# Expert weights prepared in single instructions, each behind the h of its group, and a third buffer for raw weights

## The chip, the cores and the metric

The program runs on one NeuronCore of a Trainium2 chip. The metric is the device time of one execution in microseconds (us). Three runs of the kernel before took 2126.69, 2133.93 and 2134.14 us (median 2133.93). The profile is that of one further execution, which took 2125.07 us.

Five engines work side by side, each through its own queue in order: PE (matrix multiply; PEld is its weight load), DVE (vector), ACT (activation), POOL (a second elementwise engine) and SP, which here only issues DMAs. An instruction that waits holds up all that stands behind it in its queue.

## The reference

Three layers follow one another on 2304 tokens of width 512: windowed attention, a feed-forward layer with a rational activation, and a mixture of eight experts in which every token goes through every expert:

```
P = exp(x @ w_gate - max);  8 times: P /= P.sum(1); P /= P.sum(0); P *= N / E
for e in range(8):
    h = maximum(x @ w1[e], 0)        # 512 -> 1024
    out += P[:, e:e+1] * (h @ w2[e]) # 1024 -> 512
```

The inputs and the output are float32, w1 and w2 have 2 MB each for an expert.

## The kernel before, in words

Only the expert stage, the last two thirds of the time, is touched by the change, with the end of the rational layer ahead of it.

**Groups.** The expert stage consists of 288 groups: eight experts, nine pairs of token tiles for each, four groups (i = 0 to 3) for each pair. In a group, `moe_l1` (L787) multiplies 256 tokens by two blocks of w1 in float16, each operand split into a high and a low half (24 matmuls of 256 columns, or 48 of 128 where the two tiles don't lie side by side: three pairs of the nine). `moe_a` then makes the group's h: ACT takes the relu (L804, four blocks of 128x128), POOL forms four sums and differences of the blocks (L806), ACT writes the high halves of the seven blocks that are used (L808) and DVE the low halves (L809, tile `hs`). `moe_l2` multiplies them by the prepared w2 of the group: seven block products instead of eight (`PRODS`), three matmuls each (L827 to L829), summed over i = 0 to 3 in four banks of PSUM. After the last group of a pair `y_evac` empties the four banks (ACT L860, DVE seven times L865) and adds the scaled result to the output tiles (DVE L873). All four banks are in use, so the next pair's first `moe_l2` waits for this evacuation bank by bank. In the code `moe_l2` runs two groups behind `moe_l1`.

**Preparation.** While one expert is computed, the next one's weights are made ready. Each of its eight raw tiles (128x1024 float32; k = 0 to 3 are w1, k = 4 to 7 are w2) is loaded twice. The first time DVE takes the largest absolute value (`raw_absmax`, L736). When all eight are done, `raw_scale` makes two powers of two from them. The second time the tile is split into float16 halves: for w1 one high half on ACT (L141) and one low half on DVE (L144); for w2 POOL first forms four differences of its quarters (L762, into the upper half of the tile `w4f`), then ACT and DVE split three raw quarters and the four differences apart. `raw_split` issues all of that for one tile in a row.

**Buffers.** The raw tiles share two buffers, tags `av0` and `av1`; a load is issued when the use two places ahead in the list `use` is issued. The prepared tiles rotate over six slots each for w1 and w2, four of which the running expert holds, so that i = 2 and 3 of the next expert can be written only after the running expert's last pair has used i = 0 and 1.

**Order.** The table `slots` (four slots to a group) sets the order in which the code issues the work, and `use` the groups at which the preparation is issued. The framework then schedules: it orders each engine's queue when the program is built, by a timeline of its own and by priorities, so an instruction that is issued late can be put earlier in its engine's queue where that timeline has a gap. Slots of the expert stage get a higher priority, those with `raw_absmax` and `raw_split` don't (`run_slot`, L997). Names that the prediction uses: "expert 0" to "expert 7" are the experts by number; the boundary between two experts is the first L827 of the later one.

Of the kernel before, what the change touches and what calls it, by code (L numbers as in the profile page):

```python
# [28 lines left out]
def kernel(  # L29
# [14 lines left out]
    nc = tc.nc  # L44
# [5 lines left out]
    P = 128  # L50
    KD = DM // P
# [15 lines left out]
    sb = ctx.enter_context(tc.tile_pool(name="sb", bufs=1))  # L67
# [551 lines left out]
    x2f, x2 = {}, {}  # L619
# [77 lines left out]
    NS1 = NB * NF1  # L697
# [16 lines left out]
    W1_AT = ("x1_1", "x1_2", "aqT", "aq", "ak", "x1_0")  # L714
    W2_AT = ("R0", "R1", "R2", "R3", "W5", "W6")
    ring = [0]

    def raw_load(e, k):
        t = sb.tile([P, 1024], F32, tag=f"av{ring[0] % 2}", name="wraw")
        ring[0] += 1  # L720
        w, i = divmod(k, NP)
        if w == 0:
            for h in range(2):
                nc.sync.dma_start(
                    out=t[:, h * DM:(h + 1) * DM].rearrange("p (k c) -> p k c", k=KD),
                    in_=bass.AP(w1.tensor, e * DM * FE + i * P + h * FH, [[FE, P], [P * FE, KD], [1, P]]),
                )
# [159 lines left out]
    LAG = 3  # L887
# [44 lines left out]
    after = []  # L932
# [24 lines left out]
    for n in range(NB):  # L957
        s = 4 * (SEQ.index((n, NF1 - 1, False, True)) + 1 + LAG)
# [11 lines left out]
    w4f = None  # L970
# [21 lines left out]
    for x, (s, fn, e, kx) in enumerate(use):
        at(s, fn, e, kx)
        if x + 2 < len(use):
            at(s, raw_load, *use[x + 2][2:])
# [129 lines left out]
```

## Time and profile before

| | |
|---|---|
| profiled execution | 2125.07 us, span 2123.2 us |
| PE busy | 2000.6 us (94% of the span) |
| DVE, ACT, POOL busy | 1343.0, 1022.7, 886.2 us (63%, 48%, 42%) |
| mean granted TensorE clock | 0.973 |
| DMA queue of the loads | 17.9% of the 16 engines' span |

PE's 94% is a mean over stages. The span in 40 slices (53 us each) shows PE at 6 to 8 tenths in the first five slices, where attention runs, and at 9 from there on; DVE at 8 or 9 in slices 4 to 12 and at 4 to 7 in the expert stage, which begins in slice 13. A matmul's row gives its start and a modelled end, and rows that follow each other overlap, so time that PE loses is read from the starts of rows, not from the busy share.

### The profile page before, as it was taken

How to read it: one execution, taken by the hardware profiler on the slowest of the kernel's cores; microseconds unless marked ns; L12 is line 12 of the kernel's file. 1: busy time of each engine (PE TensorE's matmuls, PEld its weight loads, DVE VectorE, ACT ScalarE, POOL GpSimd, SP SyncE). 2: the span in 40 equal slices, each digit the busy share in tenths (PEclk: the TensorE clock that was granted, in tenths of full speed). 3: DMA queues.
4: the chain of work that ended last, by engine and by line, in shares of the span. 5: the costliest groups of instructions: out<-in, count | busy, mean ns of one | idle time of the engine just before them, and what ended most of it. 6: DMA issues, size and time to landing. Idle time of an engine off the chain costs nothing.

```text
span 2123.2 us, 46647 instructions
## 1 busy us (share of the span) xinstructions
PE 2000.6 (94%) x19068; PEld 1744.0 (82%) x19068; DVE 1343.0 (63%) x2437; ACT 1022.7 (48%) x1981; POOL 886.2 (42%) x1471
## 2 busy tenths in 40 slices
PE   6688899999999999999999999999999999999998
PEld 5466678777778898989889888988988898899997
DVE  5799989989987635555554655455465555545444
ACT  5778777867863444334333333334333333334332
POOL 1222422212354534464453446455444645535333
PEclk7789999999999999999999999999999999999999
DMA  6642311131030104001210401121040112100000
GB/s 168 183 121 79 87 25 26 25 96 51 11 100 12 41 1 120 20 23 52 69 41 1 120 6 36 51 71 41 1 120 2 41 46 75 41 2 21 31 31 31
DMA packets 171654, 112.61 MB, mean 53 GB/s; under 512 B 74160, under 2 KB 156080, under 8 KB 171440
## 3 DMA queue, kind: packets, MB, share of 16 engines
q1 hardware_dynamic: 171440, 109.64, 17.9%
q8 instruction: 149, 2.44, 0.5%
q14 instruction: 65, 0.53, 0.1%
HBM read 104.88 MB, written 4.72 MB: 52 GB/s over the span
## 4 chain that ended last, share of the span: by engine, by line
PE 49%; DVE 10%; DMA 8%; POOL 5%; ACT 3%; issue 2%; SPq 1%; DVEq 0%; POOLq 0%; ACTq 0%
PE h2ps L787 25%; DMA wraw<-in_moe_w_dram 8%; PE yps L827 8%; PE yps L829 8%; PE yps L828 8%; POOL w L762 3%; DVE sm L736 2%; POOL ht L806 2%; DVE hs L809 1%; DVE ys L865 1%; ACT w1t L141 1%; DVE w1t L144 1%; DVE slab_q L576 1%; ACT hs L808 1%; DVE slab_t L588 1%
## 5 line engine op out<-in xcount | busy, mean ns | idle before, releaser
L806 POOL TENSOR_TENSOR ht<-ht 128x128 f32<-128x128 f32 x1152 | 590.6, 532 | 735.1 <-ACT ht L804 713.6
L787 PE MATMUL h2ps<-x,w1t 128*128 128x256 f16 (+1 forms) x9216 | 822.7, 247 | 0.0
L787 PEld LDWEIGHTS <-w1t 128*128 128x128 f16 x9216 | 721.0, 98 | 59.7 <-issue 0.8
L809 DVE TENSOR_TENSOR hs<-ht,hs 128x896 f16<-128x896 f32 x288 | 319.1, 1108 | 491.9 <-ACT hs L808 490.7
L827 PE MATMUL yps<-w2t,hs 128*128 128x256 f16 x2016 | 549.9, 274 | 43.5 <-DVE ys L865 39.9
L808 ACT ACTIVATE hs<-ht 128x896 f16<-128x896 f32 x288 | 273.2, 949 | 581.7 <-POOL ht L806 581.7
L828 PE MATMUL yps<-w2t,hs 128*128 128x256 f16 x2016 | 550.2, 274 | 0.0
L829 PE MATMUL yps<-w2t,hs 128*128 128x256 f16 x2016 | 547.4, 274 | 0.1
L804 ACT ACTIVATE ht<-h2ps 128x512 f32<-128x512 f32 x288 | 170.0, 590 | 237.1 <-PE h2ps L787 230.3
L828 PEld LDWEIGHTS <-hs 128*128 128x128 f16 x2016 | 197.8, 98 | 61.0 <-issue 38.2
L827 PEld LDWEIGHTS <-hs 128*128 128x128 f16 x2016 | 197.8, 98 | 33.0 <-ACT hs L808 10.6
L829 PEld LDWEIGHTS <-hs 128*128 128x128 f16 x2016 | 198.1, 98 | 24.4 <-DVE hs L809 0.6
L596 POOL TENSOR_TENSOR slab_g<-slab_t,slab_g 128x384 fp32r<-128x384 f32 x96 | 107.5, 1122 | 231.2 <-ACT slab_g L595 188.4
L865 DVE TENSOR_TENSOR ys<-yps,ys 128x256 f32<-128x256 f32 x468 | 167.2, 415 | 55.8 <-ACT ys L860 50.6
L611 PE MATMUL o1ps<-slab_g,wo_hi 128*128 128x384 f32 x384 | 139.3, 363 | 2.2 <-POOL slab_g L596 2.0
L558 PE MATMUL h1ps<-x,wi 128*128 128x384 f16 x384 | 129.4, 337 | 7.1 <-ACT p L316 4.9
L612 PE MATMUL o1ps<-slab_g,wo_lo 128*128 128x384 f32 x384 | 132.2, 344 | 0.0
L560 PE MATMUL h1ps<-x,wi 128*128 128x384 f16 x384 | 129.1, 336 | 1.0 <-DVE wi L144 0.8
L559 PE MATMUL h1ps<-x,wi 128*128 128x384 f16 x384 | 128.9, 336 | 0.0
L610 PE MATMUL o1ps<-slab_g,wo_hi 128*128 128x384 f32 x384 | 102.7, 368 | 13.7 <-ACT slab_g L595 13.2
L736 DVE TENSOR_REDUCE sm<-wraw 128x1 f32<-128x1024 f32 x64 | 77.9, 1216 | 51.1 <-DMA wraw<-in_moe_w_dram 51.0
L322 POOL TENSOR_TENSOR p<-p,sx 128x288 f32<-128x288 f32 x48 | 36.6, 762 | 128.2 <-DVE sx L321 95.7
(143 smaller groups left out, 2387.4 us busy)
## 6 DMA issues: line engine op xcount, KB each, us to landing
wraw<-in_moe_w_dram SPq DMA_DIRECT2D x192, 256.0 KB
wraw<-in_moe_w_dram SPq DMA_DIRECT2D x128, 128.0 KB
wst<-in_moe_w_in_dram SPq DMA_DIRECT2D x16, 512.0 KB
wost<-in_moe_w_out_dram SPq DMA_DIRECT2D x16, 512.0 KB
vst<-in_v_dram SPq DMA_DIRECT2D x6, 768.0 KB
out_dram<-acc SPq DMA_DIRECT2D x16, 256.0 KB
qks<-in_q_dram SPq DMA_DIRECT2D x16, 144.0 KB
qks<-in_k_dram SPq DMA_DIRECT2D x16, 144.0 KB
```

What stands on the lines that cost most here:

```text
L558: mm = nc.tensor.matmul(hp, whi, xb[:, 0, kk, :], start=kk == 0, stop=False)
L611: nc.tensor.matmul(ob[dd], hi, d["gl"], start=False, stop=False)
L612: nc.tensor.matmul(ob[dd], lo, d["gh"], start=False, stop=last)
L787: nc.tensor.matmul(hp[:, o:o + x.shape[-1]], w[:, wh, half, kk, :], x[:, xh, kk, :], start=half == 0 and kk == 0 and wh == 0 and xh == 0 a ...
L804: nc.scalar.activation(E[:, 0:4, :].rearrange("p n c -> p (n c)"), hp, AF.Relu)
L806: nc.gpsimd.tensor_tensor(out=E[:, o, :], in0=E[:, x, :], in1=E[:, y, :], op=op)
L808: nc.scalar.activation(hh, E[:, 1:8, :], AF.Copy)
L809: nc.vector.tensor_tensor(out=hl, in0=E[:, 1:8, :], in1=hh, op=ALU.subtract)
L827: nc.tensor.matmul(o, hh[:, a - 1, :], w[:, m, 0, :], start=i == 0 and half == 0, stop=False)
L828: nc.tensor.matmul(o, hh[:, a - 1, :], w[:, m, 1, :], start=False, stop=False)
L829: nc.tensor.matmul(o, hl[:, a - 1, :], w[:, m, 0, :], start=False, stop=i == NP - 1 and (half == 1 or b == 3))
L865: nc.vector.tensor_tensor(out=o, in0=s0, in1=s1, op=ALU.add)
```

## The change

`raw_split` no longer issues a tile's whole preparation. It returns a list of its single ACT and DVE instructions, which `raw_part` issues one at a time; POOL's differences are issued singly by `raw_diff`. Each of them, and each absolute maximum, gets a dependency (`pin`) on the latest instruction of the last `moe_a` on its own engine, so that the scheduler can't put it ahead of that group's h. The list of places is new: for the next expert the maxima are one to a group (before: one to a group and a half), the split starts two groups earlier and its parts are spread over several groups. From the raw tile number 20 on a third buffer, tag `x2f`, joins the two, and a load is issued at the use three places ahead. The arithmetic and the count of instructions on every engine are the same.

```diff
+    behind = {}
+    def pin(eng, i):
+        if eng in behind:
+            tc.add_manual_dep(i.ins, behind[eng], mybir.DependencyInfo(mybir.DependencyClass.Sync, mybir.DependencyReason.DATA), reason="after this group's h")
     def raw_load(e, k):
-        t = sb.tile([P, 1024], F32, tag=f"av{ring[0] % 2}", name="wraw")
+        n = ring[0]
         ring[0] += 1
+        tag = f"av{n % 2}" if n < 20 else ("av0", "av1", "x2f")[(n - 20) % 3]
+        t = sb.tile([P, 1024], F32, tag=tag, name="wraw")
...
     def raw_absmax(e, k):
-        nc.vector.tensor_reduce(out=rmx[:, k:k + 1], in_=raw.pop((e, k)), axis=AX, op=ALU.max, apply_absolute_value=True)
+        pin("v", nc.vector.tensor_reduce(out=rmx[:, k:k + 1], in_=raw.pop((e, k)), axis=AX, op=ALU.max, apply_absolute_value=True))
...
-            for o, x, y in ((d[:, 0], b[:, 0], b[:, 1]), (d[:, 1], b[:, 3], d[:, 0]), (d[:, 2], b[:, 3], b[:, 0]), (d[:, 3], b[:, 2], d[:, 1])):
-                nc.gpsimd.tensor_tensor(out=o, in0=x, in1=y, op=ALU.subtract)
-            split16(b[:, 1:4, :], t[:, 0:3, 0, :], t[:, 0:3, 1, :], e2[:, c:c + 1])()
-            split16(d, t[:, 3:7, 0, :], t[:, 3:7, 1, :], e2[:, c:c + 1])()
+            parts = [(b[:, 1:4, :], t[:, 0:3, 0, :], t[:, 0:3, 1, :], e2[:, c:c + 1]), (d, t[:, 3:7, 0, :], t[:, 3:7, 1, :], e2[:, c:c + 1])]
+        def hi(x, h, l, sc):
+            pin("a", nc.scalar.activation(h, x, AF.Copy, scale=sc))
+        def lo(x, h, l, sc):
+            pin("v", nc.vector.scalar_tensor_tensor(out=l, in0=x, scalar=sc, in1=h, op0=ALU.mult, op1=ALU.subtract))
+        return [lambda f=f, a=a: f(*a) for f in (hi, lo) for a in parts]
+    def raw_diff(e, i, o, x, y):
+        b = raw[e, NP + i].rearrange("p (n x) -> p n x", n=4)
+        d = w4f[:, 1024:2048].rearrange("p (n x) -> p n x", n=4)
+        pin("p", nc.gpsimd.tensor_tensor(out=d[:, o], in0=b[:, x], in1=d[:, y] if o % 2 else b[:, y], op=ALU.subtract))
...
-        nc.vector.tensor_tensor(out=hl, in0=E[:, 1:8, :], in1=hh, op=ALU.subtract)
+        behind["v"] = nc.vector.tensor_tensor(out=hl, in0=E[:, 1:8, :], in1=hh, op=ALU.subtract).ins.name
...
-        use += [(4 * (s0 + 3) + 6 * k + 1, raw_absmax, e, k) for k in range(8)]
-        use += [(4 * (s0 + s) + 1, raw_split, e, k) for s, k in ((18, 0), (20, 4), (22, 1), (24, 5), (33, 2), (35, 6), (36, 3), (37, 7))]
+        for i in range(8):
+            absmax_at(s0 + 4 * (4 + i) + 1, e, i)
...
+        split2_at(s0 + 4 * 36 + 3, e, 3, 1, s0 + 4 * 38 + 1, 1)
...
+    for x in range(2, len(use)):
+        s, e, kx, first = *use[x], begin[use[x]]
+        s = 4 * (NS1 + LAG + 3) if x == 22 else use[x - 2 if x < 22 else x - 3][0]
+        assert s < first
+        at(s, raw_load, e, kx)
```

What the scheduler makes of it is seen in the queues. First, DVE's queue at the boundary between experts 0 and 1, as it was: L809 is the low half of a group's h, L736 an absolute maximum for expert 2, L144 a low half of expert 1's last weights, L865 the evacuation of expert 0's last pair.

```order
L809 TENSOR_TENSOR hs<-ht,hs 128x896
L144 SCALAR_TENSOR_TENSOR w2t<-wraw,sm,w2t 128x3x256
L736 TENSOR_REDUCE sm<-wraw 128x1
L144 SCALAR_TENSOR_TENSOR w2t<-w_6335,sm,w2t 128x4x256
L736 TENSOR_REDUCE sm<-wraw 128x1
L809 TENSOR_TENSOR hs<-ht,hs 128x896
L736 TENSOR_REDUCE sm<-wraw 128x1
L865 TENSOR_TENSOR ys<-yps,ys 128x256
L865 TENSOR_TENSOR w_6335<-yps,ys 128x256
L865 TENSOR_TENSOR ys<-yps,ys 128x256 x2
L736 TENSOR_REDUCE sm<-wraw 128x1
L865 TENSOR_TENSOR acc_7138<-yps,ys 128x256
```

The same place in the changed kernel, where L835 is the h, L743 the maximum, L773 the low half of weights and L891 the evacuation:

```order
L773 SCALAR_TENSOR_TENSOR w2t<-w_6335,sm,w2t 128x4x256
L835 TENSOR_TENSOR hs<-ht,hs 128x896
L891 TENSOR_TENSOR ys<-yps,ys 128x256 x3
L891 TENSOR_TENSOR w_6335<-yps,ys 128x256
L891 TENSOR_TENSOR acc_7138<-yps,ys 128x256
L891 TENSOR_TENSOR w_6335<-yps,ys 128x256
L891 TENSOR_TENSOR acc_7138<-yps,ys 128x256
L835 TENSOR_TENSOR hs<-ht,hs 128x896 x2
L773 SCALAR_TENSOR_TENSOR w2t<-wraw,sm,w2t 128x3x256
L773 SCALAR_TENSOR_TENSOR w2t<-w_6335,sm,w2t 128x4x256
L835 TENSOR_TENSOR hs<-ht,hs 128x896 x2
L743 TENSOR_REDUCE sm<-wraw 128x1
```

The maxima have left the boundary: the first one stands behind the h of the new expert's fifth group, and nothing stands between the h and the evacuation of the old expert's last pair.

Second, POOL's queue where the first two w2 tiles of expert 1 are prepared during expert 0, as it was (L806 are the sums of h, four to a group; L762 the differences of raw weights):

```order
L806 TENSOR_TENSOR ht<-ht 128x128 x45
L762 TENSOR_TENSOR w_6335<-wraw 128x256 x2
L762 TENSOR_TENSOR w_6335<-wraw,w_6335 128x256
L806 TENSOR_TENSOR ht<-ht 128x128 x2
L762 TENSOR_TENSOR w_6335<-wraw,w_6335 128x256
L806 TENSOR_TENSOR ht<-ht 128x128 x5
L762 TENSOR_TENSOR w_6335<-wraw 128x256 x2
L806 TENSOR_TENSOR ht<-ht 128x128
L762 TENSOR_TENSOR w_6335<-wraw,w_6335 128x256 x2
```

And as it is in the changed kernel (L831 for h, L780 for the differences):

```order
L831 TENSOR_TENSOR ht<-ht 128x128 x64
L780 TENSOR_TENSOR w_6335<-wraw 128x256
L780 TENSOR_TENSOR w_6335<-wraw,w_6335 128x256
L831 TENSOR_TENSOR ht<-ht 128x128 x4
L780 TENSOR_TENSOR w_6335<-wraw 128x256
L780 TENSOR_TENSOR w_6335<-wraw,w_6335 128x256
L831 TENSOR_TENSOR ht<-ht 128x128 x20
L780 TENSOR_TENSOR w_6335<-wraw 128x256
L780 TENSOR_TENSOR w_6335<-wraw,w_6335 128x256
```

Differences now come two at a time behind a whole h and no longer split one; before, three came in a row and three more stood inside the four sums of two groups.

Third, DVE's queue at the end of the rational layer (L578 to L588 are its elementwise steps), as it was:

```order
L586 SCALAR_TENSOR_TENSOR slab_q<-slab_q,slab_a 128x384
L587 SCALAR_TENSOR_TENSOR slab_a<-slab_q,slab_a 128x384
L736 TENSOR_REDUCE sm<-wraw 128x1
L587 SCALAR_TENSOR_TENSOR slab_a<-slab_q,slab_a 128x384
L588 SCALAR_TENSOR_TENSOR slab_t<-slab_t,sm,slab_a 128x384
L119 TENSOR_REDUCE sm<-sm 128x1
L588 SCALAR_TENSOR_TENSOR slab_t<-slab_t,sm,slab_a 128x384
L736 TENSOR_REDUCE sm<-wraw 128x1 x2
L809 TENSOR_TENSOR hs<-ht,hs 128x896
```

And in the changed kernel:

```order
L586 SCALAR_TENSOR_TENSOR slab_q<-slab_q,slab_a 128x384
L587 SCALAR_TENSOR_TENSOR slab_a<-slab_q,slab_a 128x384
L588 SCALAR_TENSOR_TENSOR slab_t<-slab_t,sm,slab_a 128x384
L835 TENSOR_TENSOR hs<-ht,hs 128x896 x2
L639 TENSOR_REDUCE sm<-x2f 128x1
L773 SCALAR_TENSOR_TENSOR w2t<-wraw,sm,w2t 128x3x256
L773 SCALAR_TENSOR_TENSOR w2t<-w_6335,sm,w2t 128x4x256
L105 TENSOR_REDUCE sm<-mxps 128x1
```

All eight maxima for expert 1, and the last w2 tile of expert 0, stood in the rational layer; the maxima now stand in expert 0, one behind each h from its fifth group on, and the w2 tile behind the first two h. Ahead of the first of these maxima the queues are the same.

## Rows read from the trace of the kernel before

**Rows 1.** Waits of PE, 620 us to the end: us in total, times, longest
```profile
PE yps L827 <- DVE ys L865: 39.9, 21, 4.2
```

**Rows 2.** Busy time by stretch, experts 0, 1, 6, 7: start:end, length, PE, PEld, DVE, ACT, POOL, clock
```profile
637.16:827.48 190.32, 181.19 (x1933) 164.18 (x1934) 110.39 (x219) 81.01 (x114) 89.45 (x160) 0.98 0.12 36
827.48:1014.61 187.13, 180.15 (x1912) 163.54 (x1912) 98.17 (x152) 70.04 (x96) 91.83 (x160) 0.99 0.16 47
...
1762.59:1946.51 183.92, 181.48 (x1912) 164.34 (x1911) 94.93 (x151) 68.54 (x93) 90.17 (x160) 0.98 0.10 31
1946.51:2123.20 176.69, 169.87 (x1838) 155.28 (x1835) 74.69 (x122) 56.79 (x78) 63.06 (x137) 0.99 0.08 28
```

**Rows 3.** Timeline, undisturbed groups of expert 1: start, us, engine, line, tiles, idle before
```profile
872.41 2.84 PE L787 MATMUL h2ps<-x,w1t 128*128 128x128 f16 x48
877.38 2.78 PE L787 MATMUL h2ps<-x,w1t 128*128 128x256 f16 x24
880.87 1.81 POOL L806 TENSOR_TENSOR ht<-ht 128x128 f32<-128x128 f32 x4 [3.10 <-ACT ht L804]
882.29 2.78 PE L787 MATMUL h2ps<-x,w1t 128*128 128x256 f16 x24
882.72 0.95 ACT L808 ACTIVATE hs<-ht 128x896 f16<-128x896 f32 x1 [1.92 <-POOL ht L806]
883.70 1.09 DVE L809 TENSOR_TENSOR hs<-ht,hs 128x896 f16<-128x896 f32 x1 [3.82 <-ACT hs L808]
...
885.11 0.60 ACT L804 ACTIVATE ht<-h2ps 128x512 f32<-128x512 f32 x1 [1.45 <-PE h2ps L787]
...
886.18 2.61 DVE L865 TENSOR_TENSOR ys<-yps,ys 128x256 f32<-128x256 f32 x7 [1.39 <-ACT ys L860]
```

**Rows 4.** Timeline, DVE and PE at the boundary of experts 0 and 1
```profile
823.75 1.22 DVE L736 TENSOR_REDUCE sm<-wraw 128x1 f32<-128x1024 f32 x1 [1.48 <-DMA wraw<-in_moe_w_dram]
...
827.01 0.42 DVE L865 TENSOR_TENSOR ys<-yps,ys 128x256 f32<-128x256 f32 x1
827.48 0.37 PE L827 MATMUL yps<-w2t,hs 128*128 128x256 f16 x1 [4.22 <-DVE ys L865]
```

**Rows 5.** Busy time by stretch, the same boundary
```profile
820.00:830.00 10.00, 5.78 (x43) 4.53 (x42) 7.23 (x10) 4.10 (x6) 6.68 (x12) 0.84 0.70 206
```

**Rows 6.** Timeline, POOL, ACT and PE where expert 2's weights are split
```profile
902.73 3.19 POOL L762 TENSOR_TENSOR w<-wraw 128x256 f32<-128x256 f32 x2 [1.42 <-DMA wraw<-in_moe_w_dram]
...
908.86 1.15 ACT L141 ACTIVATE w2t<-w,sm 128x1024 f16<-128x1024 f32 x1 [4.22 <-POOL w L762]
...
912.98 0.27 PE L827 MATMUL yps<-w2t,hs 128*128 128x256 f16 x1 [2.24 <-DVE ys L865]
```

**Rows 7.** Timeline, DVE and PE at the start of the expert stage
```profile
637.21 1.22 DVE L736 TENSOR_REDUCE sm<-wraw 128x1 f32<-128x1024 f32 x1 [3.84 <-DMA wraw<-in_moe_w_dram]
...
637.16 0.28 PE L827 MATMUL yps<-w2t,hs 128*128 128x256 f16 x1 [2.34 <-ACT hs L808]
```

**Rows 8.** Busy time by stretch: five gate groups of expert 0; two stretches of the rational end
```profile
664.68:690.24 25.56, 25.56 (x332) 24.12 (x331) 19.92 (x58) 8.12 (x11) 8.87 (x20) 1.00 0.01 2
588.00:629.80 41.80, 39.90 (x257) 30.69 (x254) 41.44 (x58) 25.49 (x48) 18.35 (x17) 1.00 0.35 104
609.59:634.70 25.11, 23.08 (x158) 19.02 (x155) 21.14 (x31) 12.72 (x26) 8.29 (x12) 1.00 0.43 128
```

**Rows 9.** Groups by line, all absolute maxima of raw weights: count, busy us, mean ns
```profile
L736 DVE TENSOR_REDUCE sm<-wraw 128x1 f32<-128x1024 f32 x64 | 77.9, 1216 | 51.1 <-DMA wraw<-in_moe_w_dram 51.0
```

**Rows 10.** Timeline, first issue of a raw w2 tile on SP, and the maximum that reads it
```profile
829.97 0.34 SPq L730 DMA_DIRECT2D wraw<-in_moe_w_dram  x1
...
834.24 1.22 DVE L736 TENSOR_REDUCE sm<-wraw 128x1 f32<-128x1024 f32 x1 [2.23 <-DMA wraw<-in_moe_w_dram]
```

**Rows 11.** Timeline, a difference on POOL alone; an h on DVE beside one
```profile
908.11 0.72 POOL L762 TENSOR_TENSOR w<-wraw,w 128x256 f32<-128x256 f32 x1
...
903.84 1.50 DVE L809 TENSOR_TENSOR hs<-ht,hs 128x896 f16<-128x896 f32 x1
```

More of the change, by code (lines that the diff above doesn't have):

```diff
@@ L749, in raw_split @@
         w, i = divmod(k, NP)
-        slot = (e * NP + i) % 6
         c = e % 2
@@ L753, in raw_split, with raw_part @@
         if w == 0:
-            t = w1s[e, i] = sb.tile([P, 2, 2, KD, P], F16, tag=W1_AT[slot], name="w1t")
+            t = w1s[e, i] = sb.tile([P, 2, 2, KD, P], F16, tag=W1_AT[(e * NP + i) % 6], name="w1t")
             v = t.rearrange("p s h k c -> p s (h k c)")
-            split16(src, v[:, 0, :], v[:, 1, :], e1[:, c:c + 1])()
+            parts = [(src, v[:, 0, :], v[:, 1, :], e1[:, c:c + 1])]
         else:
-            t = w2s[e, i] = sb.tile([P, 7, 2, EH], F16, tag=W2_AT[slot], name="w2t")
+            t = w2s[e, i] = sb.tile([P, 7, 2, EH], F16, tag=W2_AT[(e * NP + i) % 6], name="w2t")
             b = src.rearrange("p (n x) -> p n x", n=4)
             d = w4f[:, 1024:2048].rearrange("p (n x) -> p n x", n=4)
-            for o, x, y in ((d[:, 0], b[:, 0], b[:, 1]), (d[:, 1], b[:, 3], d[:, 0]), (d[:, 2], b[:, 3], b[:, 0]), (d[:, 3], b[:, 2], d[:, 1])):
-                nc.gpsimd.tensor_tensor(out=o, in0=x, in1=y, op=ALU.subtract)
-            split16(b[:, 1:4, :], t[:, 0:3, 0, :], t[:, 0:3, 1, :], e2[:, c:c + 1])()
-            split16(d, t[:, 3:7, 0, :], t[:, 3:7, 1, :], e2[:, c:c + 1])()
+            parts = [(b[:, 1:4, :], t[:, 0:3, 0, :], t[:, 0:3, 1, :], e2[:, c:c + 1]), (d, t[:, 3:7, 0, :], t[:, 3:7, 1, :], e2[:, c:c + 1])]
[8 more added lines that the diff above has]
+        pin("p", nc.gpsimd.tensor_tensor(out=d[:, o], in0=b[:, x], in1=d[:, y] if o % 2 else b[:, y], op=ALU.subtract))
+    DIFFS = ((0, 0, 1), (1, 3, 0), (2, 3, 0), (3, 2, 1))
+    todo_w = {}
+    def raw_part(e, k, n):
+        if (e, k) not in todo_w:
+            todo_w[e, k] = raw_split(e, k)
+        for _ in range(n):
+            todo_w[e, k].pop(0)()
     def x2_tile(tt):
@@ L805, in moe_a @@
         for o, x, y, op in ((4, 0, 2, ALU.add), (5, 4, 1, ALU.subtract), (6, 1, 0, ALU.subtract), (7, 3, 5, ALU.subtract)):
-            nc.gpsimd.tensor_tensor(out=E[:, o, :], in0=E[:, x, :], in1=E[:, y, :], op=op)
+            i = nc.gpsimd.tensor_tensor(out=E[:, o, :], in0=E[:, x, :], in1=E[:, y, :], op=op)
+        behind["p"] = i.ins.name
         hh, hl = hs[st % 3]
-        nc.scalar.activation(hh, E[:, 1:8, :], AF.Copy)
-        nc.vector.tensor_tensor(out=hl, in0=E[:, 1:8, :], in1=hh, op=ALU.subtract)
+        behind["a"] = nc.scalar.activation(hh, E[:, 1:8, :], AF.Copy).ins.name
+        behind["v"] = nc.vector.tensor_tensor(out=hl, in0=E[:, 1:8, :], in1=hh, op=ALU.subtract).ins.name
         cur[NS1 + st] = hh, hl
@@ L976, with used, absmax_at, split1_at @@
     at(4 * 87, w4_alloc)
-    use = [(4 * (65 + k) + 1, raw_absmax, 0, k) for k in range(8)]
-    use += [(4 * (74 + i) + 1, raw_split, 0, i) for i in range(4)]
-    use += [(4 * s + 1, raw_split, 0, 4 + i) for i, s in enumerate((88, 90, 93, 96))]
+    use, begin = [], {}
+    def used(s0, s, e, kx):
+        use.append((s, e, kx))
+        begin[s, e, kx] = s0
+    def absmax_at(s, e, k):
+        at(s, raw_absmax, e, k)
+        used(s, s, e, k)
+    def split1_at(s, e, i, gap):
+        at(s, raw_part, e, i, 1)
+        at(s + gap, raw_part, e, i, 1)
+        used(s, s + gap, e, i)
+    def split2_at(s, e, i, step, t, gap):
+        for n, d in enumerate(DIFFS):
+            at(s + n * step, raw_diff, e, i, *d)
+        at(t, raw_part, e, NP + i, 1)
+        at(t + gap, raw_part, e, NP + i, 1)
+        at(t + 2 * gap, raw_part, e, NP + i, 1)
+        at(t + 3 * gap, raw_part, e, NP + i, 1)
+        used(s, t + 3 * gap, e, NP + i)
+    for i in range(8):
+        absmax_at(4 * (65 + i) + 1, 0, i)
+    for i in range(4):
+        split1_at(4 * (74 + i) + 1, 0, i, 1)
+    for i, x in enumerate((88, 90, 93, 96)):
+        split2_at(4 * x + 1, 0, i, 0, 4 * x + 1, 1)
     at(4 * 69, raw_scale, 0, 0)
@@ L984 @@
     for e in range(1, NE):
-        s0 = NS1 + (e - 1) * EB
-        use += [(4 * (s0 + 3) + 6 * k + 1, raw_absmax, e, k) for k in range(8)]
-        use += [(4 * (s0 + s) + 1, raw_split, e, k) for s, k in ((18, 0), (20, 4), (22, 1), (24, 5), (33, 2), (35, 6), (36, 3), (37, 7))]
-        at(4 * (s0 + 15), raw_scale, e, 0)
-        at(4 * (s0 + 15) + 1, raw_scale, e, 1)
-    for _, _, e, kx in use[:2]:
-        at(4 * 62, raw_load, e, kx)
[L992 to L995, printed above, removed]
+        s0 = 4 * (NS1 + (e - 1) * EB)
+        for i in range(8):
+            absmax_at(s0 + 4 * (4 + i) + 1, e, i)
+        at(s0 + 4 * 14, raw_scale, e, 0)
+        at(s0 + 4 * 14 + 1, raw_scale, e, 1)
+        split1_at(s0 + 4 * 16 + 1, e, 0, 4)
+        split2_at(s0 + 4 * 17 + 1, e, 0, 2, s0 + 4 * 19 + 3, 2)
+        split1_at(s0 + 4 * 22 + 1, e, 1, 4)
+        split2_at(s0 + 4 * 23 + 1, e, 1, 2, s0 + 4 * 25 + 3, 2)
+        split1_at(s0 + 4 * 33 + 1, e, 2, 3)
+        split2_at(s0 + 4 * 32 + 1, e, 2, 2, s0 + 4 * 35 + 1, 1)
+        split1_at(s0 + 4 * 34 + 3, e, 3, 3)
+        split2_at(s0 + 4 * 36 + 3, e, 3, 1, s0 + 4 * 38 + 1, 1)
+    for _, e, kx in use[:2]:
+        at(4 * 62, raw_load, e, kx)
+    use.sort(key=lambda u: u[0])
+    for x in range(2, len(use)):
[3 more added lines that the diff above has]
+        at(s, raw_load, e, kx)
     def run_slot(s):
         for fn, a in slots.pop(s, ()):
-            early = fn is run_piece or fn is flush or (s >= 4 * NS1 and fn not in (raw_absmax, raw_split))
+            early = fn is run_piece or fn is flush or (s >= 4 * NS1 and fn not in (raw_absmax, raw_part, raw_diff))
             with tc.high_priority(offset=400) if early else ExitStack():
```

## The prediction

> **What bounds the kernel now.** I read the waits of PE first. In the expert stage almost all of them are one kind: the first L827 of a pair waits for DVE to empty the PSUM banks, 21 times, 39.9 us [rows 1]. Then I cut the stage at each expert's first L827 [rows 2]. Expert 7, during which nothing is prepared, takes 176.69 us with the end of the program in it; experts 1 to 6 (six of one pattern, the first and last are shown) take 183.92 to 187.63, together 1946.51 - 827.48 = 1119.03 us.
>
> The timeline gives what an undisturbed expert costs. Group starts lie 877.38 - 872.41 = 4.97 us apart with 128-column matmuls and 882.29 - 877.38 = 4.91 with 256 columns, and PE shows no wait there [rows 3]. An expert has 12 of the one and 24 of the other: 59.64 + 117.84 = 177.5 us. So experts 1 to 6 lose 1119.03 - 6 x 177.5 = 54.0 us, 9.0 each. Expert 0 takes 190.32; when it starts, four h2 blocks are already multiplied instead of the usual three, so its clean time is 177.5 - 2.7 = 174.8 and it loses 15.5. Only part of this is idle time: in the 10 us around the boundary PE is busy for 5.78 and the granted clock has a mean of 0.84, so after the wait PE runs a while at the lower of its two levels, 1.2 GHz [rows 5].
>
> Two places in an expert make the loss. At the boundary DVE stands at an absolute maximum whose tile hasn't landed (1.48 us at 823.75); the h and the evacuation are queued behind it, the evacuation starts at 827.01, and PE has waited 4.22 us by 827.48 [rows 4]. About 85 us later POOL waits 1.42 us for a raw tile and takes the first two differences in 3.19 us, ACT waits 4.22 us for the last, with the next relu behind it in its queue, and PE loses 2.24 us [rows 6].
>
> **The room in an undisturbed group** [rows 3], on which the rest hangs. The h that starts at 877.38 is finished by DVE at 883.70 + 1.09 = 884.79; PE uses it after the h2 blocks of the next two groups, at about 882.29 + 4.91 + 2.6 = 889.8. That is 5.0 us of room. The evacuation starts at 886.18 and frees the first bank after one of its seven instructions (2.61 / 7 = 0.37), needed at the same 889.8: room about 3.2 us. DVE is free from 884.79 to 886.18, ACT from 883.67 to 885.11, and POOL idles 3.10 us before each h.
>
> **The change part by part.** It adds and removes no instruction, so each edit is a shift.
>
> *Maxima behind h, one to a group.* One takes 1.22 us [rows 9] and fits into DVE's 1.39 us ahead of the evacuation; in the three groups of four without evacuation there is more. What is late next if its tile isn't there: the evacuation, from 1.39 + 3.2 - 1.22, about 3.4 us on. The tile is loaded three uses ahead: 3 x 4.91 - 1.22 = 13.5 us between the release of its buffer and its use. In the trace SP's first issue and the use are 834.24 - 829.97 = 4.3 us apart, with DVE waiting at the end of them [rows 10]. So 9 us are to spare, and the boundary's wait should go. SP's own queue holds only these loads, in the order of use, so a late release delays the later ones too; each has the same spare time.
>
> *Splits as single instructions.* DVE's part (up to 1.5 us) fits like a maximum. A high half on ACT takes 1.15 us [rows 6] against 1.44 free. In two groups of an expert two come in a row, so the next relu is some 0.7 us late, of 5.0. The worst group on DVE, the one ahead of the boundary, has three low halves behind one h, about 3.8 us; they end about where the next h is ready. Two differences on POOL take 1.44 us at their shortest [rows 11] and 3.19 at their longest [rows 6], against 3.10 idle.
>
> *The end of the preparation.* The last w2 tile is now ready behind the h of group 38 of an expert's count, about three groups later than before; PE uses it at group 41. By the times above DVE is through some 10 us after group 38 starts and PE comes 17 us after it: 7 us to spare.
>
> *Bound of these.* Nothing in the trace shows a prepared expert without a loss, so I bound what stays in experts 1 to 6: nothing at one end, 4 us each (one wait of the size at 827.48) at the other. I take 1 us each, near the clean row, since every piece is smaller than its gap; two small matmuls for the scales are in it. Gain 54.0 - 6 = 48.0 us.
>
> *Expert 0.* The maxima for expert 1 now share DVE with the gate iterations. Five such groups keep DVE busy for 19.92 of 25.56 us without them [rows 8]; five maxima add 6.1, 26.0 in all, so DVE is full there and PE must wait a little. Bounds: 0 and the 6 us of the maxima; I take 3, and 2 more for matmuls of gate and logits that are real work (an estimate from that window: 25.56 against 5 x 4.93 = 24.7, so 0.9 in five groups). The start of the stage loses its bubble, its scale and its boundary waits. Gain 15.5 - 5 = 10.5, between 6 and 14.
>
> *End of the rational layer.* DVE is busy 41.44 of 41.80 us there [rows 8]. Six maxima (7.3 us) and a w2 tile leave this stretch, and two more that held the first h back, one for 3.84 us [rows 7]. PE can win its 25.11 - 23.08 = 2.0 us of idle time [rows 8] and the 2.34 us ahead of 637.16 [rows 7]: at most 4.4. It could also be nothing, if ACT's and POOL's steps are as late as DVE's. I take 3.
>
> Sum: 48.0 + 10.5 + 3 = 61.5 us off 2125.07, so 2063.5. The three runs shown lie 1.6 to 9.1 us above the profiled execution; with waits for DMA gone I expect less scatter, and forecast **2066 us** as a median.
>
> **The lock of a port.** A difference alone takes 0.72 us; beside it an h on DVE takes 1.50 instead of 1.09 [rows 3, 11]. So POOL and DVE hold each other up, and the pins put the differences just where DVE runs its h. This is rival C. The Trainium skill ("SBUF — State Buffer", SBUF: two separate sides) says that GpSimd and a VectorE instruction with two SBUF inputs take a shared pair of ports as an exclusive lock for a whole instruction and the loser blocks; these rows agree as far as they go.
>
> **The rivals.**
> A, the forecast: the waits go, 2050 to 2080. Chance 0.76.
> B, a wait in place of the one removed: DVE or a late tile still holds up one evacuation per expert, 3 to 5 us each instead of 9. For it: DVE's queue is still in order and every part still waits for others. Against: 9 us of spare time for the tile. 2066 + 6 x 3 + 4 = 2088, between 2080 and 2105. Chance 0.13.
> C, the lock: per expert 16 differences lose up to 0.7 us and 12 low halves up to 0.4, some 16 us; if three fifths of it reached PE the gain would be gone: 7 x 9.6 = 67, so 2066 + 67 = 2133. It decides only from 3.2 us of delay in one group; two differences and one low half give at most 1.8. Chance 0.03.
> D, the preparation does not do what it says, since the scheduler's order meets late tiles elsewhere: about 2125 to 2140. The queues speak against it. Chance 0.03.
> E, slower: the last w2 tile comes after its use. It has 7 us to spare; each us beyond costs PE 7 us in all, so it eats the gain from 7 + 61.5 / 7 = 16 us of delay and at 20 us gives 2066 + 7 x 13 = 2157. For it: this tile is now prepared three groups later. Against: nothing in rows 3 or 10 is late by a third of that. Chance 0.05.
>
> **How the numbers follow.** Within 0.5% (10.7 us, about what a measurement here can tell from no change) lie C and D: same 0.05, a little of D on the slower side; E and that: slower 0.05; A and B: faster 0.90. The range: below, no waits at all and the full start, 2125.07 - 54 - 13.5 - 4.4 + 2 = 2055, and some runs under it: 2049. Above, it takes in the middle of B: 2094. A and the lower part of B hold about 0.82.
>
> **What would show it.** Right: experts 1 to 6 at 178 to 179 us each, the waits of L827 for L865 under 8 us in all, the maxima of L743 without waits for DMA, clock 1.00 at the boundaries, first L853 some 3 us earlier. Wrong: an evacuation still late at an expert's start (B), differences of 1.4 us and more in every pair (C), L853 waiting for `w2t` near group 41 (E). An expert 0 above 185 us would show the gate iterations' crowding as the next bound.

## The result and the profile after

Four runs of the changed kernel took 2059.31, 2061.48, 2061.65 and 2063.64 us, median **2061.57**; the kernel before took 2130.36 in the median of its four. The ratio is 0.967 (95% interval 0.966 to 0.969). The forecast was 2066. The profiled execution took 2059.31 us (span 2057.4), 65.8 less than that of before.

The waits of PE from 620 us to the end, in the changed kernel (us in total, times, longest):

```profile
PE smps L109 <- DVE gs L681: 1.5, 3, 0.7
PE yps L853 <- DVE ys L891: 0.2, 1, 0.2
```

The second row answers to [rows 1]: 39.9 us have become 0.2. The first is new, the small matmuls of the gate in expert 0 that wait for DVE. The stage cut at the experts' first L853, for experts 0, 1 and 6 (columns as in [rows 2]; expert 7, to the end, takes 176.64 us), with the 10 us around the boundary in front:

```profile
805.00:815.00 10.00, 10.00 (x94) 8.96 (x93) 6.48 (x10) 4.37 (x7) 8.34 (x14) 1.00 0.38 106
631.86:812.13 180.27, 178.73 (x1934) 162.59 (x1932) 111.74 (x226) 80.27 (x114) 84.92 (x159) 1.00 0.18 51
812.13:990.15 178.02, 178.02 (x1915) 162.95 (x1912) 100.28 (x150) 71.61 (x95) 86.26 (x160) 1.00 0.17 49
1702.35:1880.76 178.41, 178.18 (x1915) 162.89 (x1913) 103.09 (x155) 70.66 (x93) 88.88 (x161) 1.00 0.15 43
```

PE has no gap across the boundary and its granted clock is 1.00, where [rows 5] had 5.78 us of 10 and 0.84. Experts 1 to 6 take 178.02 to 178.41 us. The timeline around the boundary, DVE, POOL, ACT and PE of the changed kernel:

```profile
802.47 1.28 DVE L773 SCALAR_TENSOR_TENSOR w1t<-wraw,sm,w1t 128x1024 f16<-128x1024 f32 x1
803.68 1.01 DVE L773 SCALAR_TENSOR_TENSOR w2t<-wraw,sm,w2t 128x768 f16<-128x768 f32 x1
803.88 3.47 POOL L831 TENSOR_TENSOR ht<-ht 128x128 f32<-128x128 f32 x4 [3.55 <-ACT ht L829]
804.61 1.48 DVE L773 SCALAR_TENSOR_TENSOR w2t<-w,sm,w2t 128x1024 f16<-128x1024 f32 x1
807.38 0.95 ACT L834 ACTIVATE hs<-ht 128x896 f16<-128x896 f32 x1 [3.58 <-POOL ht L831]
...
808.36 1.55 DVE L835 TENSOR_TENSOR hs<-ht,hs 128x896 f16<-128x896 f32 x1 [2.28 <-ACT hs L834]
...
809.84 1.27 DVE L891 TENSOR_TENSOR ys<-yps,ys 128x256 f32<-128x256 f32 x3
...
812.13 0.27 PE L853 MATMUL yps<-w2t,hs 128*128 128x256 f16 x1
...
819.30 1.28 DVE L773 SCALAR_TENSOR_TENSOR w2t<-w,sm,w2t 128x1024 f16<-128x1024 f32 x1
...
826.87 0.27 PE L853 MATMUL yps<-w2t,hs 128*128 128x256 f16 x1
```

Here the three low halves stand behind one h, the crowded group of the prediction. Beside them POOL's four sums take 3.47 us instead of 1.81 [rows 3], and still the evacuation starts 2.3 us ahead of PE's use at 812.13: the matmul's row has no wait. Where [rows 4] had a maximum and its missing tile, nothing stands between the h and the evacuation. The last two rows give the spare time of the last w2 tile: ready at 819.30 + 1.28 = 820.58, used at 826.87, so 6.3 us.

### The profile page after: what moved, and what is told of

It reads as the page before. It is cut to its first block, busy times and chain, and to the rows that moved or that the text cites. A ratio compares the mean times of both kernels' runs of the same rounds, so it can differ in the third digit from the quotient of the medians.

```text
span 2057.4 us, 46783 instructions
## 1 busy us (share of the span) xinstructions
PE 1982.5 (96%) x19068; PEld 1738.1 (84%) x19068; DVE 1363.0 (66%) x2437; ACT 1032.2 (50%) x1981; POOL 873.8 (42%) x1471
## 4 chain that ended last, share of the span: by engine, by line
PE 76%; DVE 12%; ACT 4%; DMA 2%; SPq 2%; POOL 2%; issue 1%; DVEq 0%; POOLq 0%; ACTq 0%
PE h2ps L812 35%; PE yps L853 10%; PE yps L854 10%; PE yps L855 10%; PE o1ps L611 2%; PE o1ps L610 1%; PE o1ps L612 1%; DVE slab_q L576 1%; DVE slab_q L586 1%; PE h1ps L558 1%; PE h1ps L559 1%; POOL ht L831 1%; PE h1ps L560 1%; DVE slab_t L588 1%; DVE slab_a L587 1%
## 5 line engine op out<-in xcount | busy, mean ns | idle before, releaser
L831 POOL TENSOR_TENSOR ht<-ht 128x128 f32<-128x128 f32 x1152 | 606.8, 547 | 725.3 <-ACT ht L829 703.1
L812 PE MATMUL h2ps<-x,w1t 128*128 128x256 f16 (+1 forms) x9216 | 809.5, 246 | 0.0
L835 DVE TENSOR_TENSOR hs<-ht,hs 128x896 f16<-128x896 f32 x288 | 331.9, 1154 | 561.5 <-ACT hs L834 558.8
L853 PE MATMUL yps<-w2t,hs 128*128 128x256 f16 x2016 | 548.1, 273 | 0.2 <-DVE ys L891 0.2
L853 PEld LDWEIGHTS <-hs 128*128 128x128 f16 x2016 | 197.2, 98 | 21.8
L891 DVE TENSOR_TENSOR ys<-yps,ys 128x256 f32<-128x256 f32 x468 | 168.4, 418 | 54.9 <-ACT ys L886 47.4
L612 PE MATMUL o1ps<-slab_g,wo_lo 128*128 128x384 f32 x384 | 132.1, 344 | 0.0
L560 PE MATMUL h1ps<-x,wi 128*128 128x384 f16 x384 | 128.6, 335 | 0.8 <-DVE wi L144 0.8
L610 PE MATMUL o1ps<-slab_g,wo_hi 128*128 128x384 f32 x384 | 103.7, 368 | 12.3 <-ACT slab_g L595 11.8
L899 DVE SCALAR_TENSOR_TENSOR acc<-ys,pwt,acc 128x512 f32<-128x512 f32 x112 | 89.4, 798 | 0.0
```

The costliest lines, as they stand in the source:

```text
L612: nc.tensor.matmul(ob[dd], lo, d["gh"], start=False, stop=last)
L812: nc.tensor.matmul(hp[:, o:o + x.shape[-1]], w[:, wh, half, kk, :], x[:, xh, kk, :], start=half == 0 and kk == 0 and wh == 0 and xh == 0 a ...
L831: i = nc.gpsimd.tensor_tensor(out=E[:, o, :], in0=E[:, x, :], in1=E[:, y, :], op=op)
L835: behind["v"] = nc.vector.tensor_tensor(out=hl, in0=E[:, 1:8, :], in1=hh, op=ALU.subtract).ins.name
L853: nc.tensor.matmul(o, hh[:, a - 1, :], w[:, m, 0, :], start=i == 0 and half == 0, stop=False)
L891: nc.vector.tensor_tensor(out=o, in0=s0, in1=s1, op=ALU.add)
```

## The experiments

Every kernel was run beside the kernel before; the ratio is to that, with its 95% interval. "Loss" is the median above the changed kernel's 2061.6. The kernel before took 2127.3 to 2130.4 us (medians) beside them, so a loss of less than some 3 us can't be told from none.

| kernel | median us | ratio | loss |
|---|---|---|---|
| changed, no pins | 2103.96 | 0.988 (0.987 to 0.990) | 42.4 |
| before + third buffer | 2093.51 | 0.983 (0.982 to 0.985) | 31.9 |
| before + pins | 2071.20 | 0.973 (0.971 to 0.974) | 9.6 |
| before + pins + third buffer | 2071.00 | 0.973 (0.971 to 0.974) | 9.4 |
| changed, pins on DVE alone | 2061.61 | 0.968 (0.967 to 0.970) | 0.0 |
| changed, pins on the maxima alone | 2079.03 | 0.977 (0.975 to 0.978) | 17.5 |
| changed, splits in a row | 2068.96 | 0.971 (0.969 to 0.973) | 7.4 |
| changed, one buffer for the maxima | 2079.54 | 0.977 (0.975 to 0.978) | 18.0 |
| changed, two buffers for the maxima | 2060.14 | 0.969 (0.967 to 0.971) | -1.4 |
| changed, last w2 tile two groups later | 2062.99 | 0.969 (0.968 to 0.971) | 1.4 |
| changed, nothing prepared for experts 1 to 7 | 2055.50 | 0.967 (0.965 to 0.969) | -6.1 |

### Which part of the change does it

**No pins.** `-        if eng in behind:` `+        if False:`

> The changed kernel with the pins taken away: new table, single instructions and third buffer stay. Theory P (the pins do it: the loss came from preparation that the scheduler put ahead of an h in the queues): DVE's queue again has all eight maxima for the expert after next crowded ahead of the boundary (four within two h), and POOL has four differences in a row; most of the loss returns, 2100 to 2135 us, experts 1 to 6 at 183 to 188 us each, and waits of L853 for L891 of 25 us or more. Theory T (the third buffer does it: a tile that is loaded three uses ahead is there wherever its maximum stands): 2061 to 2070 us, maxima without waits for DMA. Theory S (the new places and single instructions do it): also 2061 to 2070 us.

2103.96 us, experts 1 to 6 at 182.3 to 184.7: theory P's time. Its waits of L853 for the evacuation, though, are 9.2 us and not 25. Two more, 5.7 us, that the view puts down to a small reduction (L119) between the evacuation's instructions belong to them, and PE's other waits, mostly for DVE, are some 14. The timeline at the boundary of experts 1 and 2 shows what such a wait is made of:

```profile
1003.45 1.09 DVE L835 TENSOR_TENSOR hs<-ht,hs 128x896 f16<-128x896 f32 x1 [1.33 <-ACT hs L834]
1004.46 2.34 DVE L743 TENSOR_REDUCE sm<-wraw 128x1 f32<-128x1024 f32 x2
1006.72 0.41 DVE L891 TENSOR_TENSOR ys<-yps,ys 128x256 f32<-128x256 f32 x1
...
1007.18 0.27 PE L853 MATMUL yps<-w2t,hs 128*128 128x256 f16 x1 [2.35 <-DVE ys L891]
```

Two maxima run back to back between the h and the evacuation, without a wait for their tiles, and PE waits 2.35 us: their 2.34. So a late tile isn't needed for a loss; the work itself, put ahead of the evacuation, is enough. Tiles are late in this kernel too, though. From 620 us:

```profile
DVE sm L743 <- DMA wraw<-in_moe_w_dram: 25.3, 28, 2.1
```

So theory T's sign, maxima without waits for DMA, failed, and this run alone doesn't divide the 42 us between late tiles and the work itself.

**The third buffer alone.** The kernel before, with `tag = f"av{n % 2}" if n < 20 else ("av0", "av1", "x2f")[(n - 20) % 3]` and loads issued three uses ahead.

> The kernel before with the third buffer and loads three uses ahead alone: old table, splits in a row, no pins. Theory P: the scheduler pulls the maxima forward until the buffers run out again, the boundary keeps its waits, 2105 to 2135 us. Theory T: tiles are in time, 2062 to 2080 us. Theory S: nothing changes, about 2130 us.

2093.51 us, below P's range and far above T's: the third buffer alone is worth some 35 us. Waits of PE and of DVE in this kernel, from 620 us:

```profile
PE yps L829 <- DVE ys L867: 17.6, 23, 2.5
...
DVE sm L738 <- DMA wraw<-in_moe_w_dram: 28.6, 32, 2.3
```

The maxima still stand at the boundary and wait for 28.6 us in all, with shorter waits than before, and the evacuation is still what PE waits for.

**The pins alone.** The kernel before, with `pin` around each maximum and each instruction of `raw_split`; table and two buffers as they were.

> The kernel before with the pins alone: old table, splits of a tile in a row, two buffers, loads two uses ahead. Theory P: the maxima move behind the h of the fifth to fourteenth group of an expert, the loads lead by 13 us and more, and nearly all of the gain is there, 2062 to 2080 us (four differences behind one h are some 3 to 4 us on POOL against 3.1 idle, so a small loss at the splits may stay). Theory T: two buffers are too few, tiles come late behind pinned places too, 2100 us or more. Theory S: the boundary is mended but the splits in a row hold up a following h in four places of an expert, 2085 to 2105 us.

2071.20 us, theory P. No maximum waits for its tile, with two buffers; the first one stands behind an expert's fourth h.

**Both, on the old table.**

> The kernel before with pins and third buffer, old table and splits in a row. The pins alone gave 2071 us with two buffers, 10 us above the changed kernel, and no maximum there waited for its tile. Theory P: with pins the third buffer has nothing left to do, and the 10 us are the splits in a row behind one h: 2069 to 2074 us. Theory T: the 10 us are tiles that come late with two buffers: 2060 to 2065 us.

2071.00 us. With pins the third buffer adds nothing: its 35 us alone and the pins' 57 (2128.70 in the runs of before beside them, less 2093.51 and 2071.20) are not to be added, they remove the same loss.

**Splits in a row.** The changed kernel, with each tile's split in one slot: `split1_at(s0 + 4 * g + 1, e, kx, 0)` and `split2_at(s0 + 4 * g + 1, e, kx - NP, 0, s0 + 4 * g + 1, 0)` for (18, 0), (20, 4), (22, 1), (24, 5), (33, 2), (35, 6), (36, 3), (37, 7).

> The changed kernel with each tile's split issued in a row again, at the groups of the old table; pins, third buffer and the new places of the maxima stay. The old table with pins and third buffer took 2071.0 us, 9.4 more than the changed kernel, with single groups of 5.3 to 5.7 us where a w2 tile's four differences and two low halves stand behind one h. Theory S (these runs in a row are the 9.4 us): 2068 to 2072 us, experts 2 to 6 at 179.5 us each and the same long groups. The rival (the spacing of the maxima, one to a group instead of one to a group and a half): 2060 to 2064 us.

2068.96 us, theory S, with experts 2 to 6 at 179.5 us. The timeline shows the step:

```profile
926.15 1.41 POOL L780 TENSOR_TENSOR w<-wraw 128x256 f32<-128x256 f32 x2
927.09 1.42 DVE L835 TENSOR_TENSOR hs<-ht,hs 128x896 f16<-128x896 f32 x1 [2.77 <-ACT hs L834]
927.52 2.97 POOL L780 TENSOR_TENSOR w<-wraw,w 128x256 f32<-128x256 f32 x2
928.60 1.31 DVE L773 SCALAR_TENSOR_TENSOR w2t<-wraw,sm,w2t 128x768 f16<-128x768 f32 x1
930.45 2.85 POOL L831 TENSOR_TENSOR ht<-ht 128x128 f32<-128x128 f32 x4
930.52 1.15 ACT L770 ACTIVATE w2t<-w,sm 128x1024 f16<-128x1024 f32 x1 [1.43 <-POOL w L780]
931.71 1.28 DVE L773 SCALAR_TENSOR_TENSOR w2t<-w,sm,w2t 128x1024 f16<-128x1024 f32 x1 [1.80 <-ACT w2t L770]
```

Two differences take 1.41 us while DVE is idle for most of the time, and 2.97 beside its h and low half. Four in a row are 4.3 us, more than POOL's gap of 3.10 [rows 3], so the next h starts late, and the low half behind them waits 1.80 us ahead of the evacuation. The Trainium skill ("SBUF — State Buffer", SBUF: two separate sides) has the pair of ports that GpSimd (POOL) and a two-input VectorE (DVE) instruction share as an exclusive lock; the trace agrees that they hold each other up, in these rows and at 803.88 above.

### Which pins

**On DVE alone.** `+        if eng == "v" and eng in behind:`

> The changed kernel with pins on DVE's preparation alone; ACT's high halves and POOL's differences are free again, and POOL has four differences in a row, ahead of the h to which they would be pinned. Theory P in its first form (two places, the boundary on DVE and the split on POOL): the boundary's part goes, the split's stays: about 2 us of wait and as much of lower clock for each of seven experts, 2070 to 2095 us. Against it (the maxima on DVE are all of it, with three buffers POOL's tiles are in time): 2060 to 2066 us.

2061.61 us: the expectation "against it". POOL's differences are pulled four in a row ahead of one h, split another, and cost PE nothing here. The pins of ACT and POOL are not needed in this kernel.

**On the maxima alone.** `pin` is taken off `hi`, `lo` and `raw_diff`.

> The changed kernel with pins on the absolute maxima alone; high halves, low halves and differences are free. Without any pin the third buffer left 42 us, with DVE's pins nothing. Theory M (the maxima at the boundary are what costs; the rest of DVE's preparation is harmless in any place): 2061 to 2065 us. Theory N (any DVE preparation that stands ahead of an h costs; the low halves are pulled four in a row behind one h some 16 groups into an expert, where the kernel without pins lost about 1.5 us an expert): the boundary is mended, that place is not, 2068 to 2080 us.

2079.03 us, theory N. No maximum waits for a tile, and experts 3 to 6 take 179.9. Where the low halves are pulled ahead, in expert 1, with what POOL and ACT do behind them and the first wait of PE:

```profile
881.30 2.48 DVE L773 SCALAR_TENSOR_TENSOR w1t<-wraw,sm,w1t 128x1024 f16<-128x1024 f32 x2 [0.61 <-ACT w1t L770]
883.70 1.01 DVE L773 SCALAR_TENSOR_TENSOR w2t<-wraw,sm,w2t 128x768 f16<-128x768 f32 x1
884.63 1.27 DVE L773 SCALAR_TENSOR_TENSOR w2t<-w,sm,w2t 128x1024 f16<-128x1024 f32 x1
885.83 1.08 DVE L835 TENSOR_TENSOR hs<-ht,hs 128x896 f16<-128x896 f32 x1
...
885.58 2.06 POOL L831 TENSOR_TENSOR ht<-ht 128x128 f32<-128x128 f32 x2 [4.91 <-ACT ht L829]
887.60 2.16 POOL L780 TENSOR_TENSOR w<-wraw 128x256 f32<-128x256 f32 x2
889.72 0.45 POOL L831 TENSOR_TENSOR ht<-ht 128x128 f32<-128x128 f32 x1
...
891.30 0.95 ACT L834 ACTIVATE hs<-ht 128x896 f16<-128x896 f32 x1 [2.70 <-POOL ht L831]
...
892.30 0.28 PE L853 MATMUL yps<-w2t,hs 128*128 128x256 f16 x1 [0.47 <-ACT hs L834]
```

Four low halves, 4.6 us, stand ahead of an h; expert 1 takes 181.3 us. So pins on the maxima are not enough, and with the low halves pinned as well the loss is gone. Through which engine it comes is not shown by that: the first h that PE waits for here, at 892.30, is late on ACT, which waits 2.70 us for POOL, where differences stand inside the four sums of that h. With the low halves free the scheduler orders POOL's queue in another way too; with pins on DVE alone POOL's four differences of this tile stand ahead of one whole h.

### Late tiles, moved work, and what is left

**One buffer for the maxima.** `+        tag = f"av{n % 2}" if n < 16 else "av0" if n % 16 < 8 else ("av1", "x2f", "av0")[(n % 8) % 3]`, and their loads one use ahead.

> The changed kernel with the tiles for the maxima of experts 1 to 7 all in one buffer (the splits rotate over three as before), so that a load can start only when the maximum ahead of it is through: 4.91 - 1.22 = 3.7 us before its use, where a load took some 4.3 us. Every engine's instructions keep their places. Theory P (it counts where a wait stands, not that there is one: behind the h there are 1.39 us and 3.2 us of room ahead of the evacuation): the maxima wait for DMA 0.5 to 1 us each, 30 to 55 us in all, as much as in the kernel before, and the time stays at 2060 to 2065 us. The rival (a wait of DVE for DMA costs wherever it stands): 2080 to 2110 us.

2079.54 us: neither. DVE, the first issue of a load on SP, and PE:

```profile
852.63 1.22 DVE L743 TENSOR_REDUCE sm<-wraw 128x1 f32<-128x1024 f32 x1 [3.15 <-DMA wraw<-in_moe_w_dram]
853.88 0.34 SPq L737 DMA_DIRECT2D wraw<-in_moe_w_dram  x1
...
857.62 1.22 DVE L743 TENSOR_REDUCE sm<-wraw 128x1 f32<-128x1024 f32 x1 [2.56 <-DMA wraw<-in_moe_w_dram]
858.76 2.60 DVE L891 TENSOR_TENSOR ys<-yps,ys 128x256 f32<-128x256 f32 x7
...
860.75 0.27 PE L853 MATMUL yps<-w2t,hs 128*128 128x256 f16 x1 [0.54 <-DVE ys L891]
```

And the waits of DVE from 620 us:

```profile
DVE sm L743 <- DMA wraw<-in_moe_w_dram: 71.6, 27, 4.2
```

The maxima wait 71.6 us for DMA, more than in the kernel before (51.0 in the whole run [rows 9]), and the loss is a quarter of before's 69. So it does count where a wait stands. But I had priced each wait by itself, and the room is shared: load and maximum form a chain (from 853.88 to 857.62 + 1.22: 4.96 us; the next two take 6.3 and 6.4, the first of them because its maximum stands behind the evacuation) that is longer than a group of 4.91, so DVE falls back group by group until 3 to 5 us of room are gone, and then PE waits.

**Two buffers for the maxima.** `("av1", "av0")[n % 2]` for them; the queues of PE, DVE, ACT and POOL are those of the changed kernel.

> As the kernel with one buffer for the maxima, but with two of them: a load can start when the maximum before the last is through, 2 x 4.91 - 1.22 = 8.6 us before its use. PE, DVE, ACT and POOL have the very queues of the changed kernel, only the loads come later. With one buffer the chain of load (3.7 to 5.1 us by the trace) and maximum (1.22) was longer than a group of 4.91, so DVE fell back group by group; with two a load runs beside a maximum. Theory P: no lag builds up, hardly a wait for DMA, 2060 to 2064 us. If lateness of any size costs: between 2064 and 2079 us. If 2060 to 2064, the maxima need two buffers, not the third.

2060.14 us, theory P: no wait of a maximum for DMA from 620 us on. So the maxima don't need the third buffer. The splits of the new table have up to three tiles in hand at once; no run takes it from them, so that they need it is argued, not shown.

**The last w2 tile two groups later.** `-split2_at(s0 + 4 * 36 + 3, e, 3, 1, s0 + 4 * 38 + 1, 1)` `+split2_at(s0 + 4 * 38 + 3, e, 3, 1, s0 + 4 * 40 + 1, 1)`

> The changed kernel with each expert's last w2 tile prepared two groups later (9.8 us). In the changed kernel it was ready at 820.6 and used at 826.9, so there were 6.3 us to spare and the tile now comes 3.5 us late in each of seven experts. The scheduler sees it too and lets PE multiply part of the next h2 block (some 1.8 to 2.6 us) ahead of that place. If each us of lateness that remains costs PE a us: between 7 x 0.9 and 7 x 3.5 us, 2067 to 2086 us. If the spare time was misread (more of it): 2061 to 2064 us; if the wait also lowers the clock and makes the evacuation late: over 2090 us.

2062.99 us, below what I expected of a late tile. DVE and PE at the place:

```profile
826.13 4.53 PE L812 MATMUL h2ps<-x,w1t 128*128 128x256 f16 x40
830.50 0.38 PE L853 MATMUL yps<-w2t,hs 128*128 128x256 f16 x2
...
830.74 1.48 DVE L773 SCALAR_TENSOR_TENSOR w2t<-w,sm,w2t 128x1024 f16<-128x1024 f32 x1
```

The low half ends at 832.22, 3.5 us after the place where the changed kernel used it (826.87, and 1.89 for expert 1's later start in this run). But the scheduler put 40 h2 matmuls there instead of 24 and broke the products up among further ones; an expert takes 178.5 us instead of 178.1.

**Nothing prepared.** Experts 1 to 7 take `w1s[0, i]` and `w2s[0, i]`, and their preparation is left out.

> The changed kernel without any preparation for experts 1 to 7: these use expert 0's weights, so 56 maxima, seven eighths of the loads, splits and differences in the expert stage and the small matmuls for seven experts' scales are left out. It shows what is left to win in the preparation. If the pinned preparation costs PE nothing, only the small matmuls go (6 x 0.5 us) and most of the gate's 1.5 us of waits: 2056 to 2060 us. If loads, ports or banks still slow PE or the h chain unseen: 2050 us or less.

2055.50 us, half a microsecond under the range for a preparation that costs PE nothing. Experts 0 and 1 of this kernel, cut at the first L853 (experts 1 to 6 take the same):

```profile
632.16:809.67 177.51, 177.51 (x1930) 162.30 (x1928) 90.17 (x194) 73.59 (x106) 66.39 (x144) 1.00 0.01 2
809.67:987.24 177.57, 177.57 (x1910) 162.48 (x1908) 71.91 (x117) 59.29 (x82) 64.60 (x144) 1.00 0.01 2
```

A clean expert takes 177.57 us. The changed kernel's 178.02 is 0.45 above it, which is the group with the small matmuls for the two scales (5.36 us instead of 4.91). What is left of the preparation is 6 us: 2.8 in expert 0 and 0.45 to 0.84 in each of six others. Of the kernels that prepare everything, none is faster than the changed one by more than the measurement can tell.

## Why the prediction was right, and where it was off

**Clean cost and experts 1 to 6: right.** 177.5 us was worked out, 177.57 measured without preparation. The gain was to be 48.0 us, with 1 us an expert left; the six take 1880.76 - 812.13 = 1068.63 us instead of 1119.03 [rows 2], a gain of 50.4, with some 0.6 left.

**Expert 0: right.** Gain 10.5 forecast, 190.32 - 180.27 = 10.05 measured. Its two sizes as well: I took 3 us for the gate's crowding and 2 for real matmuls; against the kernel without preparation expert 0 takes 180.27 - 177.51 = 2.8 more, 0.45 of it the scales, and 177.51 is 2.7 above the clean 174.8. The wait that shows of it is L109's 1.5 us.

**End of the rational layer: the mis-sized term.** I took 3 us, with a bound of 4.4. The two traces are best set side by side from the last matmul L560 of that layer to the first product of expert 0. Of before:

```profile
609.43:637.16 27.73, 23.36 (x159) 19.11 (x156) 21.30 (x31) 15.29 (x29) 8.93 (x13) 1.00 0.44 133
```

and of after:

```profile
608.70:631.86 23.16, 22.21 (x158) 19.12 (x157) 13.62 (x21) 12.87 (x25) 11.24 (x17) 1.00 0.00 1
```

It is 27.73 - 23.16 = 4.6 us, and the same stretch takes 23.2 us in four of the kernels that share the changed one's queues there, so this is no scatter. PE's idle time falls from 4.37 to 0.95, which is 3.4; I had counted only the idle time on the page, and taken two thirds of it. The other 1.2 us are no matmuls that pass faster: both stretches have the same 96 h2 and 60 o1 matmuls (L610 to L612), at 0.27 and 0.34 to 0.36 us each. A break costs PE more than the idle time shown, which counts from the modelled end of a row. Of before, the same four L610, with a wait behind them and without:

```profile
629.88 0.97 PE L610 MATMUL o1ps<-slab_g,wo_hi 128*128 128x384 f32 x4
631.03 0.44 PE L611 MATMUL o1ps<-slab_g,wo_hi 128*128 128x384 f32 x1 [0.18 <-POOL slab_g L596]
...
632.54 0.87 PE L610 MATMUL o1ps<-slab_g,wo_hi 128*128 128x384 f32 x4
633.25 0.34 PE L611 MATMUL o1ps<-slab_g,wo_hi 128*128 128x384 f32 x1
```

From start to start it is 1.15 us against 0.71, so the break costs 0.44 and shows 0.18. PE waits six times in this stretch before and twice after; four breaks fewer, at some 0.26 us each that the idle time doesn't show, are 1.0 of the 1.2 (an estimate from these rows). A further 0.7 us is a lead that after has at 609 us already, where kernels with the same queues differ by 5 us.

**Sum.** 50.4 + 10.05 + 4.6 + 0.7, and 0.05 in expert 7, is the 65.8 us between the profiled executions; 61.5 was forecast. The median lay 2.3 us above the profiled execution, as allowed for.

**The cause: half right.** The step that failed in part is "At the boundary DVE stands at an absolute maximum whose tile hasn't landed". Late tiles are one share of it: the third buffer alone takes 35 us off. But without pins and with three buffers 42 us stay; tiles are still late there (25.3 us of waits), and at a boundary two maxima that wait for nothing hold up the evacuation by their own 2.34 us. With DVE's pins both go. So the common cause at the boundary is preparation on DVE that the scheduler puts ahead of h and evacuation; a late tile makes it longer. The working of the prediction, which asked only whether each tile comes in time, gave the right time because the pins take away both.

**The second place: open.** I named POOL's wait and ACT's wait behind it [rows 6] as the cause of the loss there. The trace of before bears that out for the one place:

```profile
910.04 1.28 DVE L144 SCALAR_TENSOR_TENSOR w2t<-w,sm,w2t 128x1024 f16<-128x1024 f32 x1 [3.30 <-ACT w2t L141]
910.39 0.94 ACT L808 ACTIVATE hs<-ht 128x896 f16<-128x896 f32 x1
911.36 1.23 DVE L809 TENSOR_TENSOR hs<-ht,hs 128x896 f16<-128x896 f32 x1
```

ACT, late by its wait for POOL, ends the high half of the h at 911.33; DVE's low half of weights is through at 911.32, so it isn't what the h and the evacuation behind it wait for. But the remedy need not be on POOL: with pins on DVE alone, POOL still has four differences in a row and PE loses nothing. With DVE's low halves free 17.5 us come back; whether by the low halves themselves or by the order of ACT and POOL that comes with them isn't told apart. POOL's four differences do cost something once the pins put them behind the h: in a row 7.4 us, which the finer table saves.

**The rivals.** B: waits of L853 for L891 are 0.2 us, so no new wait came. C: the hold-up between POOL and DVE is there, 3.47 us for 1.81, and finds 5.0 us of room; with the splits in a row the whole loss, of which it is a part, is 7.4 us, a tenth of what C priced. D: the order did what it says. E: the 7 us to spare were 6.3; "each us beyond costs PE 7 us in all" is wrong, since the scheduler moves other matmuls into the gap: with the tile two groups later the time rises by 1.4 us, within what can be told, and an expert by 0.4 in the traces.

## What to carry to other kernels

Where a scheduler may move low-priority work ahead in a queue that is served in order, tie that work behind the step of the main chain that it must not hold up; here it was enough to do so on one engine, the one that empties the bound engine's buffers. Before a buffer is added for late loads, ask whether the reader stands in the right place: pinned, on the old table, two buffers did as well as three, and unpinned, three did not help enough. Room in one group pays for one wait; a chain that is longer than a group uses it up in a few groups.

## What the runs showed that was not expected

Two remedies of the same wait overlap: pins alone take 57 us off and the third buffer alone 35, together on the old table 58. The new table without pins is worse than the old one without them, with three buffers each: 2103.96 to 2093.51 us. And two differences on POOL take 1.41 or 2.97 us, by what DVE does beside them.
